# Half-sequence loads, mask constants copied one pair at a time, and zero matmuls in TensorE's gaps, in an attention and MLP kernel ordered by a planner

## The chip, the core and the metric

One core of one Trainium2 chip. The core has five instruction queues that run side by side and meet through semaphores: TensorE (PE, matmuls and transposes), VectorE (DVE), ScalarE (ACT), GpSimd (POOL) and SyncE (SP, which here only issues DMAs). Each queue is in order: an instruction that waits holds everything behind it. The metric is the device time of one execution in microseconds (us).

## What is computed

Chunked top-k causal attention over 4 batches of 8 heads (768 positions, 64 wide), followed by an MLP with ELU over the 3072 tokens. The softmax's maximum and the small constant in its divisor are left out here.

```python
ub  = sum(maximum(q * k_min, q * k_max))         # bound of each query against 24 chunks of 32 keys
sel = the 6 chunks with the largest ub that are not in the future
p   = exp(scale * q @ k.T) where sel and causal, else 0
x   = (p / p.sum()) @ v                          # heads side by side: [3072, 512]
h   = x @ w_in                                   # [3072, 2048]
g   = where(h > 0, h, exp(min(h, 0)) - 1)
out = g @ w_out                                  # [3072, 512]
```

## The kernel before

The work is cut by batch b (4), half of the queries h (2 halves of 384) and head pair r (4). For each (b, h, r) the function `prep` loads keys, queries and values, transposes them on PE (f32, three 128x128 transposes, L435), takes minimum and maximum of the keys per chunk on DVE (L454, tile kmm) and from them the operand kst (L469, L476), and writes the transposed keys and queries as bf16 into the tiles lhs and rhs. `select` then works on two pairs at once: four f32 matmuls give ub (L525), DVE transposes it (L536), finds the sixth largest per query (L545), compares (L551), transposes back (L557) and writes the result into the upper half of rhs (L565). The upper half of lhs holds constants, the same for every pair: the tile econst is copied into it by DVE (L418, one copy of 64x1536 for each of the eight lhs buffers). So one score matmul (L591) gives scores and mask together. ACT takes the exponential (L603, L609; tile pt), DVE multiplies the diagonal blocks by a triangle (L618, L626), PE multiplies by v (L645), DVE normalises (L656, L659), PE transposes (L670) and DVE stores the tile xt (L675). Four tiles xt, one for each pair, are the input of one MLP stage of 384 tokens.

An MLP stage has 16 first matmul groups (L687, four matmuls of 384 columns each), an exponential on ACT (L695), a subtraction on POOL (L699, tile m), a combination on DVE (L703, tile gT), and 3 x 16 second matmuls of 512 columns (L714), evicted by ACT (L722) and stored by SP. There are eight such stages, and attention of later halves runs between them.

Loads in before: batch 0 comes as half sequences (96 KB for one head of one tensor), batches 1 to 3 as whole ones (192 KB for keys and queries, 384 KB for two heads of values). There are three buffers each for keys, queries and values, each for a whole sequence of a pair, so the keys of a fourth pair wait until both halves of the first have been transposed. SP issues them, and also the stores, in one queue; the first queries go through ACT's queue. The weights come in eight DMAs on POOL's queue (L323, L329), each planned behind one of the casts of v on POOL (L502), which a table W_GATE names.

The order of instructions on every queue is made at build time by a small planner (`Graph.run`): it walks through modelled time, with a cost in ns for each operation and engine, and lets each engine take the available operation with the smallest `prio`. `prio` is a due time in us: attention of a half, its preparation PREPAHEAD earlier, its loads LOADAHEAD earlier still, the MLP stages by MLP0 and MLPW. The kernel then emits instructions in the planned order. At the start, 28 matmuls of 128 columns on a tile of zeros (L299) stand ahead of everything on PE.

Of the kernel before, what the change touches and what calls it, by code (L numbers as in the profile page):

```python
# [20 lines left out]
D = 64  # L21
# [6 lines left out]
P = 128  # L28
# [11 lines left out]

class Buf:
# [14 lines left out]
class Op:  # L56
    __slots__ = ("name", "engines", "emit", "deps", "nexts", "bufs", "prio", "seq", "wait",
                 "ready", "start", "finish", "engine", "xfer", "gate")


class Graph:
# [13 lines left out]
    def op(self, name, engines, emit, reads=(), writes=(), prio=0.0, xfer=None, after=()):  # L75
# [5 lines left out]
        o.gate = None  # L81
# [20 lines left out]
    def run(self, at=None, dma_lat=(900.0, 1500.0)):  # L102
# [6 lines left out]
        dma_free = 0.0  # L109
# [7 lines left out]
        while left:  # L117
# [5 lines left out]
            while events and events[0] <= t:  # L123
                heapq.heappop(events)
            while arriving and arriving[0][0] <= t:
# [4 lines left out]
            while moved:  # L130
                moved = False
                for e in engines:
# [28 lines left out]
                    o.engine, o.start = e, t  # L161
                    at[e] = t + dur
                    if o.xfer is not None:
                        begin = max(t + dur + dma_lat[0], dma_free)
                        dma_free = begin + o.xfer
                        o.finish = dma_free + dma_lat[1]
                    else:
                        o.finish = t + lat
                    heapq.heappush(events, at[e])
                    for b in o.bufs:  # L170
# [4 lines left out]
                        b.left -= 1  # L175
                        b.end = max(b.end, o.finish + SEM)
                        if b.cls == "bank":
                            b.used[e] = o.finish + SEM
                            heapq.heappush(events, o.finish + SEM)
                        if b.left == 0 and b.cls in free:  # L180
                            free[b.cls].append((b.end, b.slot))
                            heapq.heappush(events, b.end)
                    for n in o.nexts:
                        n.wait -= 1
                        n.ready = max(n.ready, o.finish + SEM)
                        if n.wait == 0:
                            heapq.heappush(arriving, (n.ready, n.seq, n))
                            heapq.heappush(events, n.ready)
# [33 lines left out]
def kernel(  # L222
# [30 lines left out]
    for h in range(2):  # L253
        slots(f"rhs{h}", 5, [P, 2, HS], BF16)
# [117 lines left out]
    def load(b, h, r, prio):  # L372
# [19 lines left out]
        if h == 0:  # L392
            vfs[b, r] = g.buf("vf")
# [388 lines left out]
```

## Time and profile before

| | before |
|---|---|
| time, median of 3 runs | 320.09 us (318.78 to 321.11) |
| the profiled execution, its own time | 321.54 us |
| its span, first to last instruction | 319.6 us |
| PE / DVE / ACT / POOL busy | 92% / 72% / 63% / 44% of the span |
| first MLP matmul (L687) starts | 51.44 us |
| moved by DMA | 29.78 MB |

Busy times are sums of recorded lengths; matmuls are pipelined, so two records overlap and a busy PE is not a PE at its peak. The granted clock (PEclk) is 1.00 at 2.4 GHz and 0.50 at 1.2 GHz. Ahead of its first change it has no record and is shown as 1.00.

### The profile page before, as it was taken

How to read it: one execution, taken by the hardware profiler on the slowest of the kernel's cores; microseconds unless marked ns; L12 is line 12 of the kernel's file. 1: busy time of each engine (PE TensorE's matmuls, PEld its weight loads, DVE VectorE, ACT ScalarE, POOL GpSimd, SP SyncE). 2: the span in 40 equal slices, each digit the busy share in tenths (PEclk: the TensorE clock that was granted, in tenths of full speed). 3: DMA queues.
4: the chain of work that ended last, by engine and by line, in shares of the span. 5: the costliest groups of instructions: out<-in, count | busy, mean ns of one | idle time of the engine just before them, and what ended most of it. 6: DMA issues, size and time to landing. Idle time of an engine off the chain costs nothing.

```text
span 319.6 us, 6664 instructions
## 1 busy us (share of the span) xinstructions
PE 293.0 (92%) x2278; PEld 177.5 (56%) x2300; DVE 229.0 (72%) x687; ACT 201.5 (63%) x438; POOL 142.1 (44%) x298
## 2 busy tenths in 40 slices
PE   7486679899899999999999999999999999899995
PEld 6252346566457466565674655666665556564642
DVE  8986569977949846885499838977599919751730
ACT  4352489587468288687585766785676655952722
POOL 8563436773457224671286105451284304420730
PEclk9997699999999999999999999999999999999999
DMA  8899999993428466100144335000330000001002
GB/s 168 184 195 194 211 198 192 205 198 70 100 68 194 88 164 151 34 2 33 68 99 100 83 84 131 2 2 35 105 62 0 35 33 36 0 2 66 35 0 98
DMA packets 83168, 29.78 MB, mean 93 GB/s; under 512 B 75968, under 2 KB 80064, under 8 KB 83136
## 3 DMA queue, kind: packets, MB, share of 16 engines
q1 hardware_dynamic: 77312, 24.78, 33.3%
q0 software_dynamic: 4224, 4.19, 8.8%
q10 hardware_dynamic: 1600, 0.39, 0.6%
q8 instruction: 18, 0.29, 0.4%
q14 instruction: 14, 0.11, 0.1%
HBM read 27.26 MB, written 6.29 MB: 105 GB/s over the span
## 4 chain that ended last, share of the span: by engine, by line
PE 56%; DVE 35%; ACT 3%; issue 2%; POOL 2%; POOLq 0%; ACTq 0%; DVEq 0%
PE bank L714 23%; PE bank L687 13%; PE bank L591 9%; DVE gT L703 8%; DVE kmm L454 5%; PE bank L645 4%; PE bank L525 4%; DVE thr L545 3%; PE bank L435 2%; DVE rhs L565 2%; DVE lhs L418 2%; ACT pt L603 2%; DVE kst L476 2%; DVE qr L492 2%; DVE ubT L536 2%
## 5 line engine op out<-in xcount | busy, mean ns | idle before, releaser
L699 POOL TENSOR_SCALAR m<-e 128x384 f32<-128x384 f32 x128 | 66.1, 523 | 78.3 <-ACT e L695 57.4
L603 ACT ACTIVATE pt<-bank 128x384 bf16<-128x384 f32 (+1 forms) x160 | 74.9, 542 | 35.0 <-PE bank L591 34.2
L687 PE MATMUL bank<-xt,w_in_sb 128*128 128x384 bf16 x512 | 93.2, 326 | 0.2
L714 PE MATMUL bank<-w_out_sb,gT 128*128 128x512 bf16 x362 | 91.4, 379 | 1.1
L703 DVE SCALAR_TENSOR_TENSOR gT<-bank,m 128x384 bf16<-128x384 f32 x128 | 67.6, 548 | 23.7 <-POOL m L699 22.0
L695 ACT ACTIVATE e<-bank 128x384 f32<-128x384 f32 x128 | 61.8, 499 | 31.4 <-PE bank L687 24.5
L687 PEld LDWEIGHTS <-w_in_sb 128*128 128x128 bf16 x512 | 48.7, 98 | 30.3 <-issue 1.9
L591 PE MATMUL bank<-rhs,lhs 128*128 128x384 bf16 (+2 forms) x288 | 55.5, 302 | 10.8 <-DVE rhs L565 6.3
L714 PEld LDWEIGHTS <-gT 128*128 128x128 bf16 x384 | 36.1, 98 | 34.3 <-issue 0.8
L445 POOL COPY lhs<-kt 64x384 bf16<-64x384 bf16 x59 | 31.8, 540 | 27.5 <-ACT kt L441 25.0
L591 PEld LDWEIGHTS <-lhs 128*128 128x128 bf16 x288 | 26.9, 101 | 27.7 <-issue 11.8
L454 DVE TENSOR_REDUCE kmm<-bank 128x12 f32<-128x384 f32 x64 | 33.4, 545 | 4.5 <-PE bank L435 3.4
L645 PEld LDWEIGHTS <-pt 128*128 128x128 bf16 x672 | 24.8, 98 | 8.4 <-issue 2.7
L722 ACT ACTIVATE o<-bank 128x512 f32<-128x512 f32 x23 | 13.8, 600 | 23.4 <-PE bank L714 19.8
L645 PE MATMUL bank<-vext,pt 128*128 128x65 bf16 x672 | 26.7, 194 | 1.2 <-DVE pt L626 1.0
L441 ACT ACTIVATE kt<-bank 128x384 bf16<-128x384 f32 x29 | 14.5, 500 | 15.7 <-PE bank L435 13.1
L445 POOL CAST rhs<-qt 64x384 bf16<-64x384 f32 x21 | 11.3, 538 | 28.8 <-ACT qt L441 19.9
L525 PE MATMUL bank<-qt,kst 128*64 128x192 f32 (+1 forms) x64 | 17.5, 474 | 6.3 <-DVE kst L476 6.2
L618 DVE TENSOR_TENSOR pt<-pt,tri 128x512 bf16<-128x512 bf16 x32 | 14.6, 455 | 10.7 <-ACT pt L603 10.7
L441 ACT ACTIVATE rhs<-qt 64x384 bf16<-64x384 f32 x40 | 20.8, 521 | 1.5 <-DVE qt L443 0.9
L609 ACT ACTIVATE pt<-bank 128x512 bf16<-128x512 f32 x32 | 19.5, 608 | 1.9 <-PE bank L591 1.8
L435 PE MATMUL bank<-ident_f,qf 128*128 128x128 f32 x96 | 17.6, 298 | 1.0 <-POOL tri L308 0.6
(58 smaller groups left out, 280.0 us busy)
## 6 DMA issues: line engine op xcount, KB each, us to landing
out_dram<-o SPq DMA_DIRECT2D x24, 256.0 KB, 2.0
kf<-in_k_dram SPq DMA_DIRECT2D x24, 192.0 KB, 3.3
qf<-in_q_dram SPq DMA_DIRECT2D x24, 192.0 KB, 3.6
vf<-in_v_dram SPq DMA_DIRECT2D x12, 384.0 KB, 4.9
w_in_sb<-in_moe_w_in_dram POOLq DMA_DIRECT2D x4, 512.0 KB, 6.2
w_out_sb<-in_moe_w_out_dram POOLq DMA_DIRECT2D x4, 512.0 KB, 7.8
kf<-in_k_dram SPq DMA_DIRECT2D x16, 96.0 KB, 2.9
vf<-in_v_dram SPq DMA_DIRECT2D x16, 96.0 KB, 3.1
```

The source lines that it names most:

```text
L441: nc.scalar.activation(out=dst(), in_=src(), func=AF.Copy)
L445: nc.gpsimd.tensor_copy(out=dst(), in_=src())
L454: nc.vector.tensor_reduce(out=ap(kmm)[:, w, :], in_=ap(bank)[:, 0:HS].rearrange("p (c w) -> p c w", w=CHUNK), axis=AX.X, op=op)
L525: nc.tensor.matmul(ap(bank)[64 * j:64 * j + 64, 0:nq], lhsT=ap(ks[b, r])[:, w].rearrange("p h c -> p (h c)"), rhs=ap(qq[b, h, r][w])[:, q0 ...
L591: nc.tensor.matmul(ap(banks[hd])[:, o + pc:o + pc + wd], lhsT=ap(ls)[:, hd, P * kb:P * (kb + 1)], rhs=ap(rs)[:, hd, c0 - HS * h:c0 - HS * ...
L603: lambda e, hd=hd, pt=pt, banks=banks, wtot=wtot: nc.scalar.activation(out=ap(pt)[:, hd, 0:wtot], in_=ap(banks[hd])[:, 0:wtot], func=AF.Ex ...
L645: nc.tensor.matmul(o3v()[:, hd, qi, :], lhsT=ap(pt)[:, hd, P * qi + off:P * qi + off + P], rhs=ap(vx[b, r])[:, kb, hd, :], start=(kb == 0) ...
L687: nc.tensor.matmul(ap(bank)[:, 0:HS], lhsT=w_in_sb[:, kk, P * fc:P * (fc + 1)], rhs=ap(xT[b, h, kk]), start=(kk == 0), stop=(kk == NKK - 1))
L695: lambda e, eb=eb, bank=bank: nc.scalar.activation(out=ap(eb), in_=ap(bank)[:, 0:HS], func=AF.Exp),
L699: lambda e, eb=eb, mb=mb: nc.gpsimd.tensor_scalar(out=ap(mb), in0=ap(eb), scalar1=-1.0, scalar2=1.0, op0=AOT.add, op1=AOT.mult),
L703: lambda e, gt=gt, bank=bank, mb=mb: nc.vector.scalar_tensor_tensor(out=ap(gt), in0=ap(bank)[:, 0:HS], scalar=0.0, in1=ap(mb), op0=AOT.max ...
L714: nc.tensor.matmul(ap(bank), lhsT=ap(gts[fc])[:, P * tt:P * (tt + 1)], rhs=w_out_sb[:, fc, :], start=(fc == 0), stop=(fc == NFC - 1))
```

## The change

**Loads.** All keys, queries and values come as half sequences of one pair, for every batch, into 6, 5 and 7 half-size buffers, and v is cast half by half. SP's queue holds 212 DMAs instead of 128.

**Mask constants.** One of two memsets of econst goes; both selections on POOL read the same half. A copy of econst into a pair's lhs is now planned behind the kst operation of the last pair but one, instead of as early as possible.

**Zero matmuls.** The 28 at the start go. Fifty operations of two 128x512 matmuls on zeros, with the lowest priority of all, are given to the planner, which puts one wherever modelled PE has nothing else.

**The planner's model.** DMA queues now share the transfer rate, and POOL holds up DVE (and DVE POOL) where both use the port to SBUF that they share: all POOL operations, and those of DVE marked port=True. Start times, costs, buffer counts and due times change with it (table T). What each engine's instructions compute stays the same.

The diff, cut to its core:

```diff
+T = dict(kf=6, qf=5, vf=7, pt=12, xt=12, gT=26, qt=3, qr=3, rhs=5, nfirst=2, vlate=4.17,
+         gate=[1, 2, 3, 4, 5, 5, 8, 11], attw=[10.3, 19.0], mlp=[14.0, 15.1], loada=18.12,
+         prepa=9.74, sela=2.41, fill=50)
...
+                    if e == POOL or (e == DVE and o.port):
+                        held = max(0.0, port_free[DVE if e == POOL else POOL] - t)
+                        dur, lat = dur + held, lat + held
+                        port_free[e] = t + dur
...
-    slots("kf", 3, [P, 6, 2, D], F32)
-    slots("qf", 3, [P, 6, 2, D], F32)
-    slots("vf", 3, [P, 2, 6, D], F32)
+    slots("kf", T["kf"], [P, 3, 2, D], F32)
+    slots("qf", T["qf"], [P, 3, 2, D], F32)
+    slots("vf", T["vf"], [P, 3, 2, D], F32)
...
-    zeros = const.tile([P, P], BF16, name="zeros")
+    zeros = const.tile([P, 512], BF16, name="zeros")
...
-        nc.vector.memset(econst[up, 0], MASKNEG)
         nc.vector.memset(econst[up, 1], MASKNEG)
-        for i in range(FILL):
-            nc.tensor.matmul(store["bank"][7][:, 0:P], lhsT=zeros, rhs=zeros, start=True, stop=True)
...
-            nc.gpsimd.affine_select(out=econst[up, hd], in_=econst[up, hd],
+            nc.gpsimd.affine_select(out=econst[up, hd], in_=econst[up, 1],
...
-             writes=[(fixed, ("wi", i))], prio=-1.0, xfer=3400.0, after=[casts[W_GATE[i]]])
+             writes=[(fixed, ("wi", i))], prio=-1.0, xfer=3400.0,
+             after=[casts[W_GATE[i] - 1]] if W_GATE[i] else [])
...
-    FILL = 28
-    AT = {PE: 3500.0, ACT: 800.0, DVE: 3200.0, POOL: 6000.0, SP: 800.0}
-    W_GATE = [2, 3, 4, 5, 6, 7, 8, 9]
+    AT = {PE: 1300.0, ACT: 800.0, DVE: 4200.0, POOL: 5600.0, SP: 800.0}
+    W_GATE = T["gate"]
...
-    LOADAHEAD = 14.0
-    PREPAHEAD = 7.0
+    LOADAHEAD = T["loada"]
+    PREPAHEAD = T["prepa"]
...
     def load(b, h, r, prio):
-        if h == 0:
-            kfs[b, r], qfs[b, r] = g.buf("kf"), g.buf("qf")
-        kf, qf = kfs[b, r], qfs[b, r]
-        first = b == 0 and h == 0 and r < 2
+        kf, qf, vf = g.buf("kf"), g.buf("qf"), g.buf("vf")
+        first = b == 0 and h == 0 and r < T["nfirst"]
         ts = slice(HS * h, HS * (h + 1))
-        for buf, src, late in ((kf, k, 0.0), (qf, q, 0.001)):
+        for buf, src, late in ((kf, k, 0.0), (qf, q, 0.001), (vf, v, T["vlate"])):
             for hd in range(2):
-                if b == 0:
-                    dma(lambda buf=buf, src=src, hd=hd: (
-                            ap(buf)[:, 3 * h:3 * h + 3, hd],
-                            src[b, 2 * r + hd, ts].rearrange("(n p) d -> p n d", p=P)),
-                        [(buf, (h, hd))], [], (-100.0 + r) if first else prio + late, 440.0,
-                        f"ld{b}{h}{r}", eng=ACT if first and late else SP)
-                elif h == 0:
-                    dma(lambda buf=buf, src=src, hd=hd: (
-                            ap(buf)[:, :, hd],
-                            src[b, 2 * r + hd].rearrange("(n p) d -> p n d", p=P)),
-                        [(buf, (hh, hd)) for hh in range(2)], [], prio + late, 880.0, f"ld{b}{r}",
-                        issue=900.0)
-        if h == 0:
-            vfs[b, r] = g.buf("vf")
-        vf = vfs[b, r]
-        if b == 0:
-            for hd in range(2):
-                dma(lambda hd=hd: (ap(vf)[:, hd, 3 * h:3 * h + 3],
-                                   v[b, 2 * r + hd, ts].rearrange("(n p) d -> p n d", p=P)),
-                    [(vf, (h, hd))], [], prio + 3.0, 440.0, f"ldv{b}{h}{r}")
-        elif h == 0:
-            dma(lambda: (ap(vf).rearrange("p g n d -> p (g n) d"),
-                         v[b, 2 * r:2 * r + 2].rearrange("g s d -> (g s) d")
-                         .rearrange("(m p) d -> p m d", p=P)),
-                [(vf, (hh, hd)) for hh in range(2) for hd in range(2)], [], prio + 3.0, 1760.0,
-                f"ldv{b}{r}", issue=900.0)
+                early = first and src is not v
+                dma(lambda buf=buf, src=src, hd=hd: (
+                        ap(buf)[:, :, hd], src[b, 2 * r + hd, ts].rearrange("(n p) d -> p n d", p=P)),
+                    [(buf, hd)], [], (-100.0 + r) if early else prio + late, 450.0,
+                    f"ld{b}{h}{r}", eng=ACT if early and late else SP)
...
-                g.op("ec" + tag, {DVE: (480, 560)}, ec, writes=[(lb, "e")],
-                     prio=prio + 0.5)
+                g.op("ec" + tag, {DVE: (480, 560)}, ec, writes=[(lb, "e")], port=True,
+                     prio=prio + 0.5, after=[ecs[-2]] if len(ecs) > 1 else [])
...
-        def cast(name, ks_, cost, keys):
-            casts.append(g.op(
-                name, cost,
-                lambda e: nc.gpsimd.tensor_scalar(
-                    out=ap(vx[b, r])[:, ks_, :, 0:D].rearrange("p k g d -> p g k d"),
-                    in0=ap(vf)[:, :, ks_], scalar1=1.0, scalar2=0.0, op0=AOT.mult, op1=AOT.add),
-                reads=[(vf, key) for key in keys], writes=[(vx[b, r], hh) for hh in {k_[0] for k_ in keys}],
-                prio=prio + 3.0))
-        if b == 0:
-            cast("v" + tag, slice(3 * h, 3 * h + 3), {POOL: (520, 580)}, [(h, 0), (h, 1)])
-        elif h == 0:
-            cast("v" + tag, slice(0, 6), {POOL: (850, 910)}, [(hh, hd) for hh in range(2) for hd in range(2)])
+        casts.append(g.op(
+            "v" + tag, {POOL: (520, 580)},
+            lambda e: nc.gpsimd.tensor_scalar(
+                out=ap(vx[b, r])[:, 3 * h:3 * h + 3, :, 0:D],
+                in0=ap(vf), scalar1=1.0, scalar2=0.0, op0=AOT.mult, op1=AOT.add),
+            reads=[(vf, 0), (vf, 1)], writes=[(vx[b, r], h)], prio=prio + T["vlate"]))
...
+    last = None
+    for i in range(T["fill"]):
+        bank = g.buf("bank")
+
+        def fill(e, bank=bank):
+            for _ in range(2):
+                nc.tensor.matmul(ap(bank), lhsT=zeros[:, 0:P], rhs=zeros, start=True, stop=True)
+        last = g.op("fill", {PE: (432, 600)}, fill, writes=[(bank, 0)], prio=1e6,
+                    after=[last] if last else [])
```

DVE's queue behind the memsets of the constants, before: copies of econst, then qr (positive part of the queries), kmm (chunk minimum and maximum of the keys) and kst.

```order
L418 COPY lhs_81<-econst 64x1536
L418 COPY lhs_82<-econst 64x1536
L418 COPY lhs_83<-econst 64x1536
L418 COPY lhs_84<-econst 64x1536
L418 COPY lhs_85<-econst 64x1536
L418 COPY lhs_86<-econst 64x1536
L418 COPY lhs_87<-econst 64x1536
L492 TENSOR_SCALAR qr_122<-qt_118 128x192
L454 TENSOR_REDUCE kmm_115<-bank_62 128x12 x2
L418 COPY lhs_88<-econst 64x1536
L476 TENSOR_TENSOR kst_107<-kmm_115,half 128x4x12
```

The same place after the change.

```order
L437 COPY lhs_90<-econst 64x1536
L437 COPY lhs_91<-econst 64x1536
L462 COPY qt_127<-bank_68 128x384
L474 TENSOR_REDUCE kmm_124<-bank_67 128x12 x2
L513 TENSOR_SCALAR qr_130<-qt_127 128x192
L462 COPY qt_128<-bank_64 128x384
L496 TENSOR_TENSOR kst_116<-kmm_124,half 128x4x12
L474 TENSOR_REDUCE kmm_125<-bank_63 128x12 x2
L513 TENSOR_SCALAR qr_131<-qt_128 128x192
L489 TENSOR_TENSOR kmm_125<-kmm_125 128x12
L474 TENSOR_REDUCE kmm_126<-bank_61 128x12
```

Two copies instead of seven stand ahead of the first kmm, and a copy of transposed queries out of PSUM (qt) has come to DVE.

PE's queue behind the first zero matmuls, before: transposes of queries and keys (qf, kf) of three pairs, then the first selection matmuls.

```order
L435 MATMUL bank_61<-ident_f,qf_72 128x128 x3
L435 MATMUL bank_62<-ident_f,kf_69 128x128 x3
L435 MATMUL bank_63<-ident_f,qf_73 128x128 x3
L435 MATMUL bank_64<-ident_f,kf_70 128x128 x3
L435 MATMUL bank_65<-ident_f,kf_71 128x128 x3
L435 MATMUL bank_66<-ident_f,qf_74 128x128 x3
L525 MATMUL bank_67<-qt_118,kst_107 64x192
L525 MATMUL bank_67<-qt_119,kst_108 64x192
```

The same place after the change: zero matmuls stand between the transposes (each with its weight load).

```order
L454 MATMUL bank_67<-ident_f,kf_69 128x128 x3
L454 MATMUL bank_68<-ident_f,qf_75 128x128 x3
L762 LDWEIGHTS zeros
L762 MATMUL bank_61<-zeros 128x512
...
L762 LDWEIGHTS zeros
L762 MATMUL bank_62<-zeros 128x512
...
L454 MATMUL bank_63<-ident_f,kf_70 128x128 x3
L454 MATMUL bank_64<-ident_f,qf_76 128x128 x3
```

Ahead of the first MLP matmul there are 82 zero matmuls of 512 columns now; up to that point PE's queue has 48 transposes instead of 60, 36 score matmuls instead of 48 and 48 matmuls with v instead of 78.

The last second matmuls (L714, L731 after the change) of the program, before.

```order
L714 LDWEIGHTS gT_170
L714 MATMUL bank_64<-w_out_sb,gT_170 128x512
L714 LDWEIGHTS gT_171
L714 MATMUL bank_64<-w_out_sb,gT_171 128x512
L714 LDWEIGHTS gT_188
L714 MATMUL bank_64<-w_out_sb,gT_188 128x512
L714 LDWEIGHTS gT_189
L714 MATMUL bank_64<-w_out_sb,gT_189 128x512
```

Near the same place after the change.

```order
L731 LDWEIGHTS gT_177
L731 MATMUL bank_66<-w_out_sb,gT_177 128x512
L731 LDWEIGHTS gT_178
L731 MATMUL bank_66<-w_out_sb,gT_178 128x512
L762 LDWEIGHTS zeros
L762 MATMUL bank_63<-zeros 128x512
...
L731 LDWEIGHTS gT_195
L731 MATMUL bank_66<-w_out_sb,gT_195 128x512
```

Two zero matmuls stand behind each of the first three groups of four of the last sixteen, six in all, and twelve more behind the last one.

## Rows read from the trace of the kernel before

**Rows 1.** The page's first part, all engines: busy us, share of the span, instructions.
```profile
PE 293.0 (92%) x2278; PEld 177.5 (56%) x2300; DVE 229.0 (72%) x687; ACT 201.5 (63%) x438; POOL 142.1 (44%) x298
```

**Rows 2.** Busy time by stretch up to the first L687; columns as in the first line.
```profile
core 0: us, PE busy (x) PEld busy (x) DVE busy (x) ACT busy (x) POOL busy (x), PEclk, DMA share, GB/s
...
26.75:30.17 3.42, 3.42 (x8) 0.97 (x6) 0.47 (x2) 0.00 (x0) 1.76 (x4) 0.50 1.08 201
...
33.58:40.41 6.83, 5.63 (x24) 3.34 (x24) 3.25 (x8) 3.49 (x8) 2.77 (x5) 0.50 1.27 211
...
sum 51.44, PE 36.35 PEld 24.20 DVE 39.28 ACT 26.07 POOL 26.72; mean PE 6.06 PEld 4.03 DVE 6.55 ACT 4.35 POOL 4.45
```

**Rows 3.** The same view for stretches behind 64 us.
```profile
64.00:305.32 241.32, 234.81 (x1894) 142.55 (x1914) 175.65 (x524) 164.44 (x361) 103.70 (x210) 1.00 0.29 69
305.32:315.88 10.56, 10.47 (x49) 4.61 (x47) 1.67 (x3) 1.79 (x4) 1.07 (x3) 1.00 0.13 50
315.88:319.60 3.72, 0.00 (x0) 0.00 (x0) 0.00 (x0) 0.60 (x1) 0.00 (x0) 1.00 0.18 70
```

**Rows 4.** Timeline of PE and DVE, 0 to 52.2 us: start, length, instructions [idle before].
```profile
1.06 3.17 PE L299 MATMUL bank<-zeros 128*128 128x128 bf16 x28 [1.06 <-DVE warm L292]
...
4.80 5.66 DVE L418 COPY lhs<-econst 64x1536 bf16<-64x1536 bf16 x7
...
10.65 1.01 DVE L454 TENSOR_REDUCE kmm<-bank 128x12 f32<-128x384 f32 x2
...
19.02 2.29 PE L591 MATMUL bank<-rhs,lhs 128*128 128x384 bf16 x10 [1.36 <-DVE rhs L565]
...
22.17 0.84 PE L435 MATMUL bank<-ident_f,kf 128*128 128x128 f32 x3
...
23.42 0.53 PE L435 MATMUL bank<-ident_f,qf 128*128 128x128 f32 x3
...
51.44 1.07 PE L687 MATMUL bank<-xt,w_in_sb 128*128 128x384 bf16 x4
...
51.80 0.34 DVE L675 COPY xt<-bank 128x384 bf16<-128x384 bf16 x1
```

**Rows 5.** Waits of DVE up to 52.2 us: us in total, times, longest.
```profile
DVE ubT L536 <- PE bank L525: 5.6, 2, 3.1
```

**Rows 6.** Groups by line and shape, DVE: busy us, mean ns | idle before.
```profile
L454 DVE TENSOR_REDUCE kmm<-bank 128x12 f32<-128x384 f32 x64 | 33.4, 545 | 4.5 <-PE bank L435 3.4 <-ACT kt L441 0.9
...
L659 DVE TENSOR_TENSOR on<-bank,rcp 128x384 bf16<-128x384 f32 x32 | 17.4, 548 | 0.3
...
L618 DVE TENSOR_TENSOR pt<-pt,tri 128x512 bf16<-128x512 bf16 x32 | 14.6, 455 | 10.7 <-ACT pt L603 10.7
...
L443 DVE CAST rhs<-qt 64x384 bf16<-64x384 f32 x3 | 2.0, 653 | 0.0
...
L297 DVE MEMSET econst<- 64x768 bf16 x1 | 0.7, 698 | 0.1
```

**Rows 7.** Chain that ended last, pieces in order of time: start, us, what.
```profile
101.96 0.66 PE bank L435 x6
...
295.73 9.75 PE bank L687 x60
...
305.75 10.11 PE bank L714 x46
```

**Rows 8.** Waits of PE from 64 us on: us in total, times, longest.
```profile
PE bank L525 <- DVE kst L476: 1.7, 2, 1.1
```

**Rows 9.** DMA: the page's issues (KB, us to landing), SP's timeline and waits.
```profile
kf<-in_k_dram SPq DMA_DIRECT2D x24, 192.0 KB, 3.3
...
w_out_sb<-in_moe_w_out_dram POOLq DMA_DIRECT2D x4, 512.0 KB, 7.8
kf<-in_k_dram SPq DMA_DIRECT2D x16, 96.0 KB, 2.9
...
12.21 1.02 SPq L369 DMA_DIRECT2D kf<-in_k_dram  x2
...
SPq L369 <- ACT o L722: 134.3, 19, 24.9
```

More of the change, by code (lines that the diff above doesn't have):

```diff
@@ L57 @@
     __slots__ = ("name", "engines", "emit", "deps", "nexts", "bufs", "prio", "seq", "wait",
-                 "ready", "start", "finish", "engine", "xfer", "gate")
+                 "ready", "start", "finish", "engine", "xfer", "port")
 class Graph:
@@ L73, in buf, with op @@
         return Buf(cls)
-    def op(self, name, engines, emit, reads=(), writes=(), prio=0.0, xfer=None, after=()):
+    def op(self, name, engines, emit, reads=(), writes=(), prio=0.0, xfer=None, after=(),
+           port=False):
         o = Op()
@@ L80, in op @@
         o.start = o.finish = o.engine = None
-        o.gate = None
+        o.port = port
         for b, key in reads:
@@ L108, in run @@
         arriving = []
-        dma_free = 0.0
+        rings = {e: [] for e in (SP, ACT, POOL)}
+        dma_at, asked = 0.0, -1.0
+        port_free = {DVE: 0.0, POOL: 0.0}
         for o in self.ops:
@@ L174, in run @@
                             b.slot = fl.pop(k)[1]
[L175 to L188, printed above, removed]
+                    if o.xfer is None:
+                        o.finish = t + lat
+                        settle(o)
+                    else:
+                        rings[e].append([t + dur + dma_lat[0], o.xfer, o])
+                        heapq.heappush(events, t + dur + dma_lat[0] + o.xfer)
                     order.append(o)
@@ L470, in sub @@
                               op=AOT.subtract)
-        g.op("ks" + tag, {DVE: (85, 160), POOL: (200, 260)}, sub, reads=[(kmm, 0)], writes=[(kmm, 1)],
-             prio=prio)
+        g.op("ks" + tag, {DVE: (75, 150), POOL: (200, 300)}, sub, reads=[(kmm, 0)], writes=[(kmm, 1)],
+             prio=prio, port=True)
         def pad(e):
@@ L621, in tri @@
                         .to_broadcast([P, 2, 2, P]), op=AOT.mult)
-                g.op("tri" + tag, {DVE: (340, 430)}, tri, reads=[], writes=[(pt, 0), (pt, 1)], prio=pr)
+                g.op("tri" + tag, {DVE: (340, 430)}, tri, reads=[], writes=[(pt, 0), (pt, 1)], prio=pr,
+                     port=True)
             elif dg:
@@ L629, in tri @@
                         op=AOT.mult)
-                g.op("tri" + tag, {DVE: (200, 290)}, tri, reads=[], writes=[(pt, 0), (pt, 1)], prio=pr)
+                g.op("tri" + tag, {DVE: (200, 290)}, tri, reads=[], writes=[(pt, 0), (pt, 1)], prio=pr,
+                     port=True)
             for (kb, c0, wd, pc) in segs:
```

100 lines of the change are left out of this document (70 added, 30 removed).

## Prediction

> **What bounds the kernel now.** I read the engine shares first, then the spans of the first 51 us, then of the rest, and then the waits of the engines that wait or are waited for. TensorE (PE) is busy 92% of the span, VectorE (DVE) 72%, ScalarE (ACT) 63%, GpSimd (POOL) 44% [rows 1]. The share alone hides that there are two kernels here. From 64.00 to 305.32 us PE is idle for 241.32 - 234.81 = 6.5 us in all, and the last stretch of second matmuls (305.32 to 315.88) is busy to 0.1 us; then 3.7 us of eviction and store follow [rows 3]. There the kernel is bound by PE, and nothing short of less matmul work moves it by more than these 6.5 us. The first 51.44 us are different: the first MLP matmul (L687) starts only then [rows 4], because its four tiles xt need attention of all four head pairs of the first half sequence. Up to there PE was busy 36.35 us and DVE 39.28 us [rows 2].
>
> Two things lengthen that stage. First, the chain runs through DVE: seven copies of the mask constants take 4.80 to 10.46 us, and the first reduction of the transposed keys stands behind them in DVE's queue [rows 4]. Second, PE works at its half level. The granted clock reads 0.50 from 26.75 to 30.17 and from 33.58 to 40.41 [rows 2]. Ahead of the first change there is no record, but the durations tell: 28 filler matmuls of 128 columns need 3.17 us, 0.11 us each; three f32 transposes need 0.84 us at 22.17 and 0.53 us at 23.42 [rows 4]. So PE was at 1.2 GHz until about 23.3, with a little work and many gaps, and rose after it had worked nearly without a break from 19.02. The page on TensorE in the Trainium skill ("TensorE: Matmul & The Clock Gate", "What's actually happening") says the same: the throttled level is the default, and activity lifts it. The trace agrees.
>
> **The change, part by part: DVE's way to the last xt.** In before, DVE had done 39.3 us of work by 51.44 and 0.8 us more when the fourth xt was done at 52.14 [rows 2, 4]: 40.1. Its order is fixed, so the list up to the fourth xt can be compared item by item. After the change it holds four mask copies instead of eight (4 x 5.66/7 = 3.2 us less), no casts of q where there were two (2 x 0.653 = 1.3), one memset of 0.70 us less, two L618 products less (0.9), and one each less of L454 and L659 (0.55 each) [rows 4, 6]; a few smaller differences, on balance in the same direction, are left out. That is 7.2 us less: 32.9 us of work. To it come the waits. Before had 52.14 - 40.1 = 12.0 us of them, of which 5.6 us were two waits for the selection matmuls (L525) [rows 5], both while the clock was 0.50 [rows 2]. In the new order some 2.5 us of DVE work stands between the operands of the first selection and its transpose, so I let these 5.6 us go, and keep the other 6.4. So the last xt is done at 32.9 + 6.4 = 39.3. Twelve score matmuls (L591) of the next half stand ahead of the first L687, so I put that at **40.0 instead of 51.44: -11.4 us**. Bounds, with the same 0.7 us behind xt: at 3.4 us of waits it starts at 37.0 (-14.4), and with all 12.0 us of before at 45.6 (-5.8).
>
> **The filler matmuls.** 82 matmuls of 128x512 on zeros stand in front of the first L687. At the spacing of the last second matmuls, 10.11/46 = 0.22 us [rows 7], they are 17.7 us of PE. With the 15.2 us of real work left there, PE is filled for 34 of the 40 us. Each us that PE begins at the half level adds half a us. That fits under the 40.0, so I cost them at nothing; what hides them is DVE's work, and if that cover is gone each costs its 0.22 us. What they buy is the clock, which is in the waits above. Six more stand between the groups of the last sixteen second matmuls. There PE had no gap (10.47 of 10.56 busy [rows 3]), so these cost their full length: 6 x 0.22 = **+1.3 us** (bounds 0, if a gT comes late there, and 1.3). The last twelve run beside the final eviction and store, in which PE idled 3.72 us [rows 3]: 2.6 us, hidden.
>
> **Work that is now done later.** Ahead of the first L687 stand 12 f32 transposes fewer, 8 score matmuls of 384 columns, 30 matmuls of probabilities with v, and a few short ones. At 0.11 us each [rows 7], 0.1625 us (the L687 row, also 384 columns [rows 7]) and an estimated 0.03 us (65/512 of the 0.22 us row) that is 1.3 + 1.3 + 0.9, with the short ones about **+4.0 us** that PE does later, in the part where it has no slack.
>
> **The full stretch.** PE's waits for DVE there are few: 1.7 us for kst is the largest [rows 8]. Prep work gets 9.74 instead of 7 us of lead and the planner now counts the port that DVE and POOL share, so I take **-2.0 us** of the 6.5 (bounds -6 and +3: a new order can also lose).
>
> **Loads.** Loads of half a sequence double the number from batch 1 on: 212 on SP's queue where there were 128. An issue of two 96 KB loads takes 1.02 us [rows 9], so 84 more are some 43 us on SP, which spends 134 us waiting for ACT's evictions ahead of its stores [rows 9]; hidden, and if that cover went they would come on top of the queue. Landing took 2.9 us for 96 KB and 3.3 us for 192 KB, both far under the lead that the buffers give [rows 9]. A rule that speaks against this part stands in "DMA: Bandwidth & Descriptors", "Rules for kernel authors": join small transfers into large ones. By the rows the sum has nothing for the halving; by the rule the second rival below, at 319.5, would be the likelier. POOL's 12 more casts of v and ACT's 11 more copies of q lie on engines at 44% and 63%.
>
> **Sum.** -11.4 + 4.0 + 1.3 - 2.0 = -8.1 us. The profiled execution had a span of 319.6 us and 321.54 us in all; the median of the runs was 320.09, 1.45 less. So the span should be 311.5 and the time **312.0 us**.
>
> **The rivals.** *DVE never waits* (chance 0.17): first L687 at 37.0, and 4 us of the 6.5 gone: -14.4 + 4.0 + 1.3 - 4 = -13.1, 307 us. For it: a clock at full level shortens every matmul that DVE waits for. Against: selections and exponentials still alternate between three engines.
>
> *Loads fall behind* (0.14): the DMA engines were taken, at a share of 1.08 and 1.27 in the two stretches of low clock [rows 2]. All eight weight loads must be in before the first MLP can finish, and each takes 7.8 us to land in this crowd [rows 9]. In PE's order the first matmul that needs the last of them stands behind some 24 us of matmuls after the first L687 (20 in before), counted with the spacings above: at 64 us instead of 71. If the pace of the loads sets the time, the gain of 8 us is waited away: about 319.5. Against it: POOL issues the weight loads earlier, and ahead of the last one stand only three quarters of batch 1's first half, not all of batch 1's keys and queries.
>
> *The clock stays low* (0.04), on the slower side. PE needs 17.7 + 15.2 us at full level from 1.1 on, 34.0. Each us at the half level does half a us, so with the first 28 us low the first L687 comes at 48, and 48 - 51.44 + 4.0 + 1.3 - 2 is zero: from there on the fillers make the kernel slower; with 40 us low it starts at 54 and the time is 326 us. For it: the fillers at the start of before did not lift the level. Against: the unbroken work from 19.02 on did [rows 4].
>
> *Loads behind stores* (0.05), slower too: SP's queue is in order, and loads of the next half stand behind stores that wait for ACT (134.3 us [rows 9]). With six buffers for keys the slack is large, but if in each of the seven later stages PE waits over 1.2 us for a load the gain is gone; at 1.6 us it ends at 323.
>
> **How the numbers follow.** My forecast has 0.60; alone it would reach from 308 to 316.5. A measurement of this kernel can tell about 1% from no change, 316.9 to 323.3. Faster: 0.60 + 0.17 = 0.77; same: 0.14; slower: 0.04 + 0.05 = 0.09. The range that leaves out no more than 2 in 10 reaches from under the first rival (its -13.1, and 1.5 more for stalls that vanish), 305.5, to the second, 319.5.
>
> **What would show it.** In the changed kernel's profile: the first reduction of keys on DVE near 7 us instead of 10.65; the granted clock at 1.00 wherever it has a record before 40 us; the first L704 (the old L687) at 37 to 45.6; DVE's wait for the selection matmuls under 2 us; six zero matmuls inside the last second matmuls with 0.22 us each; PE idle between the first 64 us and the tail at 1 to 9 us. I am wrong if the first MLP matmul is early and PE then waits for w_out or for keys, or if PE is filled but DVE is late by the old 12 us.

## The result and the profile after

The changed kernel takes 310.53 us (median; 309.59 to 311.63), the kernel before 320.6 us on the same chip: a ratio of 0.9696, with a 95% interval of 0.9642 to 0.9749. That is 10.1 us less; the forecast had 8.1 less and 312.0. Ratios here and below leave out executions over 1.5% above the fastest of their kernel, which are one each of e2 and e7 and two of e6, its profiled one among them. The profiled execution took 310.68 us, with a span of 308.6 instead of 319.6.

The total was right by luck: the two largest terms behind it were not, and their errors cancel. From the start to the first MLP matmul I had expected 11.4 us less and it became 2.6 (48.80 instead of 51.44). Behind it I had expected 2.0 us fewer stalls, and some 13.4 went. Here is how that is read.

The page of the changed kernel, engine shares and the chain that ended last:

```profile
PE 295.0 (96%) x2346; PEld 178.3 (58%) x2372; DVE 221.6 (72%) x676; ACT 204.2 (66%) x449; POOL 143.5 (46%) x309
...
PE 87%; DMA 7%; SPq 5%; issue 1%
```

Busy time by stretch, same kernel (columns as in [rows 2]); the third row answers to the first of [rows 3]:

```profile
6.03:40.17 34.14, 24.09 (x173) 14.69 (x176) 21.82 (x72) 16.48 (x35) 18.80 (x42) 1.00 1.12 196
40.17:43.58 3.41, 3.41 (x33) 1.73 (x30) 0.80 (x3) 0.23 (x1) 1.26 (x4) 0.50 0.81 184
64.00:304.92 240.92, 239.65 (x1944) 146.21 (x1965) 174.91 (x522) 168.59 (x372) 106.97 (x224) 1.00 0.29 74
304.92:308.60 3.68, 2.75 (x13) 1.08 (x11) 0.00 (x0) 0.60 (x1) 0.00 (x0) 1.00 0.18 71
```

PE is idle for 1.3 us behind 64 us, where it was 6.5. From 6.03 to 40.17 it is idle for 10 of 34.14 us, zero matmuls included among its work. What it waited for, over the whole span (us in total, times, longest):

```profile
PE bank L454 <- DMA kf<-in_k_dram: 6.0, 2, 3.1
PE bank L454 <- DMA qf<-in_q_dram: 3.9, 1, 3.9
PE bank L762 <- DVE warm L336: 1.3, 1, 1.3
PE bank L731 <- issue: 0.2, 1, 0.2
```

Three waits for keys and queries, 9.9 us, all before the first MLP matmul; before, no load stood among PE's large waits. The timeline of PE (start, length, instructions [idle before]) has them in place, with the first MLP matmul and the tail:

```profile
18.30 0.52 PE L454 MATMUL bank<-ident_f,kf 128*128 128x128 f32 x3 [2.92 <-DMA kf<-in_k_dram]
...
27.89 0.52 PE L454 MATMUL bank<-ident_f,kf 128*128 128x128 f32 x3 [3.07 <-DMA kf<-in_k_dram]
...
38.80 0.52 PE L454 MATMUL bank<-ident_f,qf 128*128 128x128 f32 x3 [3.90 <-DMA qf<-in_q_dram]
...
48.80 1.46 PE L704 MATMUL bank<-xt,w_in_sb 128*128 128x384 bf16 x8
...
301.03 0.59 PE L762 MATMUL bank<-zeros 128*128 128x512 bf16 x2
301.46 1.03 PE L731 MATMUL bank<-w_out_sb,gT 128*128 128x512 bf16 x4
```

PE takes its instructions in order. The transposes (L454) of later pairs stand ahead of score matmuls whose operands are there, so a late load stops all of PE, and DVE behind it. DVE's waits up to 52.2 us, with the row that answers to [rows 5] first:

```profile
DVE ubT L551 <- PE bank L540: 5.5, 2, 5.2
DVE rcp L673 <- PE bank L662: 5.5, 3, 4.8
DVE pt L633 <- ACT pt L618: 3.7, 2, 3.0
```

**Where the stalls behind the first MLP matmul went.** Busy time doesn't show them all: a record of L704 lasts 326 ns (page after; 95.8 us for 512), while such matmuls follow each other every 0.1625 us [rows 7], so records overlap and cover small gaps. I therefore count spacings. Before, 512 first matmuls (0.1625 us each), 384 second ones (0.216), 132 f32 transposes (0.109), 240 score matmuls (22.1, 5.7 and 2.9 us by width), the selections (14.9), 594 with v (0.0295) and 81 transposes of attention (0.056) follow the first L687: 248.1 us. From there to the end of the last second matmul (its start and one spacing) it took 264.2. So PE lost some 16.2 us, where the gaps between records add up to 7.8 (6.5 of them behind 64 us). After: 252.1 of work, 1.3 of zero matmuls, 256.1 elapsed, 2.8 lost. The table has the same count for every profiled run. It is an estimate from spacings, all at the full clock level; its columns add up to the span within 0.2 us. *Rest* is what follows the last second matmul.

| kernel | first MLP matmul at | work behind it | zeros | PE lost | rest | span | median us |
|---|---|---|---|---|---|---|---|
| before | 51.44 | 248.1 | 0 | 16.2 | 4.0 | 319.6 | 320.1 |
| changed | 48.80 | 252.1 | 1.3 | 2.8 | 3.7 | 308.6 | 310.5 |
| e1 late weights | 41.16 | 252.1 | 1.3 | 3.7 | 3.7 | 301.9 | 303.7 |
| e2 no zeros in the tail | 45.24 | 252.1 | 0 | 2.8 | 3.7 | 303.8 | 307.3 |
| e3 no zeros | 50.03 | 252.1 | 0 | 2.8 | 3.7 | 308.6 | 309.7 |
| e4 no hold on the port | 33.85 | 254.7 | 1.3 | 13.7 | 9.3 | 312.7 | 313.5 |
| e5 old due times | 46.07 | 253.7 | 1.3 | 7.9 | 4.1 | 313.0 | 313.6 |
| e6 e1 + e2 | 39.23 | 252.1 | 0 | 8.8 | 3.7 | 303.8 | 304.1 |
| e7 e1 + e3 | 39.31 | 252.1 | 0 | 2.8 | 3.7 | 297.9 | 302.8 |
| e8 before + hold | 43.33 | 249.8 | 0 | 9.2 | 4.0 | 306.3 | 308.9 |
| e9 e7, no hold | 33.57 | 254.7 | 0 | 11.6 | 3.7 | 303.5 | 304.9 |
| e10 before + copies gated | 42.50 | 250.1 | 0 | 17.2 | 4.0 | 313.8 | 315.7 |
| e11 before + due times | 41.15 | 250.7 | 0 | 12.3 | 4.3 | 308.4 | 309.7 |
| e12 before + 140 zeros | 51.51 | 248.1 | 0 | 16.1 | 4.0 | 319.6 | 321.5 |

### The profile page after: what moved, and what is told of

The parts are those of the page before. It is cut to its first block, busy times and chain, and to the rows that moved or that the text cites. A ratio compares the mean times of both kernels' runs of the same rounds, so it can differ in the third digit from the quotient of the medians.

```text
span 308.6 us, 6957 instructions
## 1 busy us (share of the span) xinstructions
PE 295.0 (96%) x2346; PEld 178.3 (58%) x2372; DVE 221.6 (72%) x676; ACT 204.2 (66%) x449; POOL 143.5 (46%) x309
## 4 chain that ended last, share of the span: by engine, by line
PE 87%; DMA 7%; SPq 5%; issue 1%
PE bank L704 27%; PE bank L731 26%; PE bank L606 11%; PE bank L662 7%; PE bank L454 6%; PE bank L540 6%; SPq L411 5%; DMA qf<-in_q_dram 4%; DMA kf<-in_k_dram 3%; PE bank L762 2%; PE bank L687 2%
## 5 line engine op out<-in xcount | busy, mean ns | idle before, releaser
L704 PE MATMUL bank<-xt,w_in_sb 128*128 128x384 bf16 x512 | 95.8, 326 | 0.0
L731 PE MATMUL bank<-w_out_sb,gT 128*128 128x512 bf16 x362 | 92.0, 379 | 1.2 <-issue 0.2
L618 ACT ACTIVATE pt<-bank 128x384 bf16<-128x384 f32 (+1 forms) x160 | 76.6, 538 | 18.3 <-PE bank L606 18.0
L704 PEld LDWEIGHTS <-w_in_sb 128*128 128x128 bf16 x512 | 48.7, 98 | 28.6 <-issue 0.6
L464 POOL COPY lhs<-kt 64x384 bf16<-64x384 bf16 x62 | 32.7, 527 | 60.1 <-ACT kt L460 58.1
L731 PEld LDWEIGHTS <-gT 128*128 128x128 bf16 x384 | 35.9, 98 | 32.5 <-issue 0.6
L606 PE MATMUL bank<-rhs,lhs 128*128 128x384 bf16 (+2 forms) x288 | 54.4, 290 | 0.1
L606 PEld LDWEIGHTS <-lhs 128*128 128x128 bf16 x288 | 25.8, 98 | 19.0 <-issue 1.7
L739 ACT ACTIVATE o<-bank 128x512 f32<-128x512 f32 x23 | 13.7, 595 | 30.5 <-PE bank L731 28.9
L460 ACT ACTIVATE kt<-bank 128x384 bf16<-128x384 f32 x32 | 15.8, 494 | 23.6 <-PE bank L454 22.8
L460 ACT ACTIVATE rhs<-qt 64x384 bf16<-64x384 f32 x51 | 26.7, 523 | 4.3 <-DVE qt L462 3.5
L662 PEld LDWEIGHTS <-pt 128*128 128x128 bf16 x672 | 24.6, 99 | 8.1 <-issue 4.7
L762 PE MATMUL bank<-zeros 128*128 128x512 bf16 x96 | 26.9, 410 | 1.4 <-DVE warm L336 1.3
L662 PE MATMUL bank<-vext,pt 128*128 128x65 bf16 x672 | 26.6, 195 | 0.0
L454 PE MATMUL bank<-ident_f,kf 128*128 128x128 f32 x96 | 15.9, 274 | 6.0 <-DMA kf<-in_k_dram 6.0
L522 POOL TENSOR_SCALAR vext<-vf 128x384 bf16<-128x384 f32 x32 | 17.2, 543 | 8.6 <-DMA vf<-in_v_dram 4.0
```

The source lines that it names most:

```text
L454: nc.tensor.transpose(ap(bk)[:, P * n:P * (n + 1)], ap(src)[:, n], ident_f)
L460: nc.scalar.activation(out=dst(), in_=src(), func=AF.Copy)
L606: nc.tensor.matmul(ap(banks[hd])[:, o + pc:o + pc + wd], lhsT=ap(ls)[:, hd, P * kb:P * (kb + 1)], rhs=ap(rs)[:, hd, c0 - HS * h:c0 - HS * ...
L618: lambda e, hd=hd, pt=pt, banks=banks, wtot=wtot: nc.scalar.activation(out=ap(pt)[:, hd, 0:wtot], in_=ap(banks[hd])[:, 0:wtot], func=AF.Ex ...
L662: nc.tensor.matmul(o3v()[:, hd, qi, :], lhsT=ap(pt)[:, hd, P * qi + off:P * qi + off + P], rhs=ap(vx[b, r])[:, kb, hd, :], start=(kb == 0) ...
L704: nc.tensor.matmul(ap(bank)[:, 0:HS], lhsT=w_in_sb[:, kk, P * fc:P * (fc + 1)], rhs=ap(xT[b, h, kk]), start=(kk == 0), stop=(kk == NKK - 1))
```

## Experiments on the start: loads, zero matmuls, clock

**e1, the weight loads later.** POOL issues the first weight load at 10.73 us in the changed kernel, at 16.69 before. In the stretch from 10 to 29 us loads of 96 KB landed slowly (DMA issues of the changed kernel in that stretch: KB, median us to landing):

```profile
w_in_sb<-in_moe_w_in_dram POOLq DMA_DIRECT2D x4, 512.0 KB, 8.2
w_out_sb<-in_moe_w_out_dram POOLq DMA_DIRECT2D x2, 512.0 KB, 9.6
vf<-in_v_dram SPq DMA_DIRECT2D x8, 96.0 KB, 7.1
kf<-in_k_dram SPq DMA_DIRECT2D x6, 96.0 KB, 5.9
qf<-in_q_dram SPq DMA_DIRECT2D x6, 96.0 KB, 6.4
```

From 64 to 290 us they take 2.4 to 2.6 us. So seven weight loads (the expectation says six) are moved later in POOL's order, five of them behind named casts of v, the last two behind another load and a kst operation:

```
 order = g.run(AT)
+for w, c in (("w_in0", "v003"), ("w_in1", "v010"), ("w_in2", "v011"), ("w_in3", "v012"),
+             ("w_out0", "v013"), ("w_out1", "w_out0"), ("w_out2", "kp013")):
+    o = next(x for x in order if x.name == w)
+    order.remove(o)
+    order.insert(next(i for i, x in enumerate(order) if x.name == c) + 1, o)
```

> The changed kernel with the same order on PE, DVE, ACT and SP; on POOL's queue six weight loads stand later (the first behind the cast of the fourth pair's v instead of the first pair's). Theory 'weights crowd the loads': in the changed kernel PE waited three times, 9.9 us in all, for keys and queries that took 6.2 to 10.1 us to land while weight loads were under way, against 2.4 to 2.9 without. These waits fall under 3 us in all, the first L704 comes at 40 to 43 us instead of 48.8, and the time at 302 to 305. Rival 'the loads' own pace is the limit' (SP issues one each 0.53 us): the waits stay above 8 us, the first L704 stays within 2 us of 48.8, the time within 309 to 312.

Measured: 303.70 us, ratio to before 0.949 (0.9435 to 0.9546). The first weight load is issued at 18.61, the first L704 starts at 41.16, and of PE's waits for loads one is left (waits of PE, e1, and from its timeline the first L704):

```profile
PE bank L454 <- DMA qf<-in_q_dram: 2.5, 1, 2.5
PE bank L762 <- DVE warm L336: 1.3, 1, 1.3
...
41.16 1.46 PE L704 MATMUL bank<-xt,w_in_sb 128*128 128x384 bf16 x8
```

The key loads of e1 issued from 10 to 18.6 us, ahead of its first weight load, and then from 18.6 to 29:

```profile
kf<-in_k_dram SPq DMA_DIRECT2D x4, 96.0 KB, 2.6
...
kf<-in_k_dram SPq DMA_DIRECT2D x4, 96.0 KB, 7.8
```

Queries went from 2.6 to 8.1 us, values from 2.6 to 6.3. So loads land as slowly beside the weights here; they are later ones, and PE stood still for only one of them. In this order of PE, the weights' early place cost the changed kernel 7 us. The Trainium skill has a rule beside this ("DMA: Bandwidth & Descriptors", "Issuing engines are not separate DMA queues"): transfers started by different engines run on the same 16 DMA engines and interleave. These rows agree.

**e2 and e3, the zero matmuls.** e2 drops those behind the last first matmul, e3 all 100:

```
 order = g.run(AT)
+last_mm = max(i for i, x in enumerate(order) if x.name.startswith("h7."))
+order = [x for i, x in enumerate(order) if x.name != "fill" or i < last_mm]    # e2
+order = [x for x in order if x.name != "fill"]                                 # e3
```

> The changed kernel without its 18 zero matmuls behind the last first matmul of the MLP (six inside the last second matmuls, twelve behind them). Theory: the six cost their full 0.216 us each, so 309.2 us (-1.3). Rival: they fill gaps that PE has anyway, no change (within 0.4 us of the changed kernel).

> The changed kernel with none of its 100 zero matmuls. Theory 'the fillers hold the clock': granted clock 0.50, or durations at the half level, over most of the stretch up to the first L704; the 15.2 us of real work in it take up to 30, the first L704 comes at 51 to 55 instead of 48.8, and with 1.3 us back in the tail the time is 311.5 to 315.5. Rival 'loads set the pace there, the clock does not matter': first L704 within 1 us of 48.8, time 309.2 (the tail alone).

Measured: e2 307.26 us (0.9580; 0.9527 to 0.9633), e3 309.71 (0.9653; 0.9589 to 0.9717). In e2 the way from the first L704 to the end is 258.5 us instead of 259.8: the tail's 1.3 us. The rest of its gain is the start, 45.24 instead of 48.80 with the very same order up to there. PE's waits for loads were 6.0 us instead of 9.9; so the landing of loads moves the start by several us between executions, and what starts less than that apart shows nothing. In e3 the half level lasts long: three f32 transposes take 0.85 to 0.90 us until the clock rises at 22.81 (0.49 to 0.55 in the changed kernel), and from there to 50.12 the granted clock averages 0.75. PE waits 12.4 us for loads, and the first L704 starts 1.2 us later. By the times, e2 and e3 differ by 2.4 us with intervals that overlap, so what the 82 early zero matmuls are worth here stays open.

**e6 and e7, both on top of e1.** With loads no longer in the way the clock could count again. e6 is e1 with e2's edit, e7 is e1 with e3's.

> The changed kernel with both things that the first runs showed to cost time taken out: weight loads later in POOL's order, and no zero matmuls behind the last first matmuls. Theory (the two are separate, 303.7 - 1.3): 302.4 us, range 301 to 303.5. Rival (the zero matmuls of the tail hide under another wait once the start is shorter): 303.7 as with the late loads alone.

> Weight loads late, and none of the 100 zero matmuls at all. Theory (with the loads early, loads set the pace of the start and the clock hardly counted; with the loads late PE's real work sets it, and the half level costs again): first MLP matmul at 44 to 48 us instead of 41.2, low clock until 20 us and longer; 305.5 to 309 us. Rival (the clock does not count here either): first MLP matmul at 40 to 42, 302.4 us or less.

Measured: e6 304.11 us (301.33 to 307.04; ratio 0.9425, 0.9377 to 0.9472), e7 302.82 (299.96 to 304.50; ratio 0.9426, 0.9369 to 0.9484), whose profiled execution is the 299.96. By the ratios they are the same, and neither is told from e1 (0.949). For e7 my theory fell and the rival held, but for 0.4 us in the time and 0.7 in the start. PE of e7:

```profile
4.26 0.88 PE L454 MATMUL bank<-ident_f,kf 128*128 128x128 f32 x3 [4.26 <-DMA kf<-in_k_dram]
...
20.93 0.85 PE L454 MATMUL bank<-ident_f,kf 128*128 128x128 f32 x3
...
24.67 0.49 PE L454 MATMUL bank<-ident_f,qf 128*128 128x128 f32 x3
...
39.31 1.46 PE L704 MATMUL bank<-xt,w_in_sb 128*128 128x384 bf16 x8
```

PE was at 1.2 GHz until after 20.93 us, and the first L704 came at 39.31 all the same, against 41.16 with 82 zero matmuls. So they buy no time that shows here: e7 is e6 without them, at the same ratio. The profiled execution of e6 took 305.93 us, so its row in the table (8.8 us lost) does not stand for the 0.9425.

**e12, zero matmuls in the kernel before.** 140 instead of 28 at the start:

```
-FILL = 28
+FILL = 140
```

> The kernel before, with 140 zero matmuls of 128 columns at its start instead of 28, and nothing else: they fill PE until the first keys and queries can be transposed and a little beyond. Theory of the forecast (PE at its half level lengthens the selections that DVE waits for): full level from some 6 us on instead of 23.3, first MLP matmul at 46 to 49 us, 315 to 318 us. Rival (loads and DVE set the pace at the start, the clock counts little): 319 us or more.

Measured: 321.52 us, 0.8% slower (1.008; 1.0047 to 1.0113). PE of e12:

```profile
1.06 9.57 PE L299 MATMUL bank<-zeros 128*128 128x128 bf16 x140 [1.06 <-DVE warm L292]
10.47 0.50 PE L435 MATMUL bank<-ident_f,qf 128*128 128x128 f32 x3
...
51.51 0.94 PE L687 MATMUL bank<-xt,w_in_sb 128*128 128x384 bf16 x4
```

The level did rise (0.50 us for three transposes instead of 0.87; the granted clock reads 1.00 from 4.42 us), and the first L687 stood where it was. As a trial of the clock alone it is not clean: the zeros also held the first transposes back from 4.79 to 10.47 us, and the level fell again at 18.1. That the clock buys nothing that shows at this start rests on e7 against e6.

## Experiments on the full stretch: the port, the due times, the mask copies

**e4 and e9, the changed kernel without the hold.** The planner no longer delays an operation for the port that DVE and POOL share; e4 is the changed kernel with this edit, e9 is e7 with it:

```
-held = max(0.0, port_free[DVE if e == POOL else POOL] - t)
+held = 0.0
```

> The changed kernel, planned without the hold of DVE and POOL on each other's port (one line of the planner), so in another order. Theory 'the port in the model took PE's stalls away': by the spacing of matmuls PE lost about 16.3 us between the first L687 and the last L714 in before and 2.7 us in the changed kernel; without the hold it loses 9 us or more there, and the time is 316 or more. Rival 'due times, buffers and half loads did it': PE loses under 5 us there, and the time is within 2 us of the changed kernel's 310.5.

> The version with late weight loads and no zero matmuls, with the planner's hold on the shared port taken out. In the earlier run without the hold 38 zero matmuls stood behind the last real one and made the run longer by themselves; here there are none, so the hold is priced cleanly. Theory (the hold takes PE's waits for DVE out): PE loses 7 us or more between first and last MLP matmul where it lost 2.8; 305.5 to 312 us. Rival (the hold buys nothing that an earlier start does not): 301.5 to 304.5 us.

Measured: e4 313.48 us (0.9789; 0.9747 to 0.9831). PE lost 13.7 us, as the theory had it, but the time is under the theory's 316 and over the rival's 312.5. Its tail and its start show that it priced something else too:

```profile
33.85 2.11 PE L704 MATMUL bank<-xt,w_in_sb 128*128 128x384 bf16 x12
...
303.48 8.37 PE L762 MATMUL bank<-zeros 128*128 128x512 bf16 x38
```

The planner had placed fewer zeros early and 38 were left for the end, some 5.6 us behind all other work (9.3 instead of 3.7 in the table). The start says more about e1. The first L704 comes 15 us earlier than in the changed kernel, although the first weight load is issued at 11.09 us, about as early, and keys issued from 10 to 29 us land in 7.4 us at the median. But 39 transposes stand ahead of it instead of 48, and 24 score matmuls instead of 36. PE waits 1.1 us for loads ahead of it, not 9.9. So slow loads need not delay the start: that depends on what stands behind them in PE's order. Hence e9, without zeros: 304.89 us (0.9550; 0.9511 to 0.9589), 2.1 us behind e7. PE lost 11.6 us instead of 2.8, as the theory wanted, and its waits for DVE are back (waits of PE in e9 from the first L704 to 300 us; e7 has none there):

```profile
PE bank L606 <- DVE gT L720: 1.5, 3, 0.7
PE bank L662 <- DVE pt L642: 1.4, 2, 0.8
PE bank L606 <- ACT kt L460: 0.9, 1, 0.9
```

But the first MLP matmul came 5.7 us earlier, with 2.6 us more work left. So the time, 304.9, lay between the theory (305.5 or more) and the rival (304.5 at most): the hold trades an early start for fewer stalls, and wins by 2 us here, or by 4 if the ratios to before are compared (0.9426 and 0.9550; e7 and e9 ran on two chips).

**e8, the hold alone in the kernel before.**

```
+port_free = {DVE: 0.0, POOL: 0.0}
...
+if e == POOL or (e == DVE and o.name.startswith(port)):
+    held = max(0.0, port_free[DVE if e == POOL else POOL] - t)
+    dur, lat = dur + held, lat + held
+    port_free[e] = t + dur
```

with port = ("ec", "ka", "ks", "kp", "qr", "qa", "lt", "mk", "tri"), the names that the change marks.

> The kernel before, with one part of the change alone: the planner holds an operation of POOL, or one of DVE that uses the shared port, until the other is done with it. Theory (that alone takes most of PE's waits for DVE out of the full stretch): of the 16.2 us that PE lost there, 6 to 12 go; 308 to 315 us. Rival (it needs the new due times or the new start): 317 us or more, with the waits for gT, xt, rhs and pt still there.

Measured: 308.87 us (0.9648; 0.9611 to 0.9685). These lines alone are worth as much as the whole change. Of the 16.2 us lost 7.0 went. PE's named waits from the first MLP matmul on fell only from 5.5 to 3.2 us (those for xt, rhs and gT are still there), so most of the 7.0 us is in stalls that no row names. The first MLP matmul came at 43.33 with 1.7 us more work behind it, although DVE's queue still begins with seven mask copies (DVE of e8):

```profile
4.80 4.73 DVE L424 COPY lhs<-econst 64x1536 bf16<-64x1536 bf16 x7
...
9.93 1.01 DVE L460 TENSOR_REDUCE kmm<-bank 128x12 f32<-128x384 f32 x2
```

**e5 and e11, the due times.** e5 gives the changed kernel the old ones; e11 gives the kernel before the new ones (the other entries of T are left out):

```
-vlate=4.17, attw=[10.3, 19.0], loada=18.12, prepa=9.74, sela=2.41
+vlate=3.0,  attw=[10.0, 19.0], loada=14.0,  prepa=7.0,  sela=2.0     # e5; e11 the other way
```

> The changed kernel with the due times of before (loads 14.0 us ahead instead of 18.12, preparation 7.0 instead of 9.74, selection 2.0 instead of 2.41, v 3.0 instead of 4.17 later, attention of the first halves 10.0 instead of 10.3 us wide); the planner still counts the port of DVE and POOL. Theory (the port in the planner takes PE's waits for DVE out of the full stretch): PE loses under 6 us there, as in the changed kernel; 309 to 312 us. Rival (the longer lead of the preparation does it): waits of PE for gT, xt, rhs and pt come back, 6 us or more; 314 to 320 us.

> The kernel before, with the new due times alone (loads 18.12 us ahead, preparation 9.74, selection 2.41 behind it, v 4.17, attention of first halves 10.3 wide), without the hold on the port. Theory (the lead alone also takes waits away, in the changed kernel it was worth some 5 us of PE's loss): PE loses 9 to 13 us behind the first MLP matmul instead of 16.2; 312 to 317 us. Rival (without the hold the planner thinks DVE is on time anyway, and three buffers of whole sequences give no more lead): 318.5 us or more.

Measured: e5 313.63 us (0.9785; 0.9727 to 0.9843), 3.1 us behind the changed kernel, with 7.9 us lost. The time lies between theory (312 at most) and rival (314 or more); the loss is of the rival's size, though the named waits that came back are mostly for ACT, not for DVE (waits of PE in e5 from the first L704 on):

```profile
PE bank L606 <- ACT pt L618: 1.5, 3, 0.7
PE bank L606 <- DVE rhs L580: 0.4, 1, 0.4
```

e11: 309.72 us (0.9714; 0.9670 to 0.9758), faster than its theory. The due times alone also bring nearly the whole gain: in the profiled execution 10.3 us from the earlier start, less 2.6 us of work moved behind it, and 3.9 us of the loss. With the hold and the due times both tried in both kernels, the rest of the change (buffers, half loads, costs, zero matmuls) shows little in the loss: 9.2 and 7.9 with the hold alone (e8, e5), 12.3 and 11.6 with the due times alone (e11, e9). The changed kernel without both was not run.

**e10, the mask copies alone.** From the third pair on a copy waits for the statistics (kst) of two calls earlier; the list ecs holds those operations (cut to the core):

```
-g.op("ec" + tag, {DVE: (480, 560)}, ec, writes=[(lb, "e")], prio=prio + 0.5)
+g.op("ec" + tag, {DVE: (480, 560)}, ec, writes=[(lb, "e")], prio=prio + 0.5,
+     after=[ecs[-2]] if len(ecs) > 1 else [])
```

> The kernel before, with one part of the change alone: from the third pair on a mask copy waits for the block statistics (kst) of two calls earlier, so two copies stand at the start of DVE's queue instead of seven. Theory (the copies hold up the first key reduction and with it the start): first reduction near 7 us, first MLP matmul 2 to 4 us earlier than 51.4; 316 to 318.5 us. Rival (the copies fill time in which DVE would have waited): 319 to 321 us.

Measured: 315.73 us (0.9880; 0.9832 to 0.9929), 0.3 us under the theory's range and clear of the rival. DVE of e10:

```profile
4.80 1.11 DVE L419 COPY lhs<-econst 64x1536 bf16<-64x1536 bf16 x2
...
6.79 1.02 DVE L455 TENSOR_REDUCE kmm<-bank 128x12 f32<-128x384 f32 x2
```

The first reduction starts at 6.79 and the first MLP matmul at 42.50, 8.9 us earlier instead of the 2 to 4 expected; but 2.0 us of work and 1.0 us of stalls move behind it. 5.8 us are left of the span, and 3.2 in the medians. The start of the MLP is not the end of the kernel, and a new order does not lower the loss by itself: it is 17.2 here.

## Why the prediction came out right, point by point

**What bounds the kernel.** Half right. The start and the full stretch do have different limits. But "nothing short of less matmul work moves it by more than these 6.5 us" failed: behind the first MLP matmul 13.4 us of stalls went with 5.3 us more for PE to do. The step that failed is taking PE's busy time as its work: a record of L704 lasts 326 ns at 162 ns of spacing. The Trainium skill ("Perfetto Trace Analysis", "Identifying the Most-Contended Engine") says that the busy share of matmuls is not a good measure of how close a kernel is to its limit (roofline), since they are pipelined. These rows agree.

**DVE's way to the last xt, -11.4.** Mis-sized, and outside its bounds: -2.6 in the profiled execution. The work was sized well (DVE was busy for 32.4 us in the first 48.80, I had 32.9; DVE's 0.8 us between 51.44 and 52.14 can only be 0.7, which changes nothing), and the first reduction came at 7.93. The waits failed. I let the 5.6 us behind the selections go and kept 6.4; in their place stand 5.5 us behind the selections and 5.5 more for L662, the longest of each behind PE's waits for loads at 38.80 and 27.89. So two of the signs that I had named did not come, the first L704 at 45.6 or earlier and a wait for the selections under 2 us. The earlier weight loads were in the diff; I set them down as an argument against the rival on loads and gave them no price. With the first weight load at 18.61 instead of 10.73 us (e1; 16.69 before) the size of the term holds: 41.16, or 39.31 in e7, for the 40.0 of the forecast.

**The zero matmuls.** That the 82 ahead of the MLP are hidden holds, and so do the 1.3 us of the tail (0.43 us for each pair; e2). That they buy time through the clock did not show: e7 against e6.

**Work done later, +4.0.** Held: 252.1 against 248.1, by the count of matmuls.

**The full stretch, -2.0.** Mis-sized. By the measure that it was given in, PE's idle time between records behind 64 us, it was -5.2 (6.5 to 1.3), within its bounds; by the spacings, which the time follows, -13.4, outside them. Both the hold and the due times feed it: with the hold alone the loss falls from 16.2 to 9.2 (e8), with the due times alone to 12.3 (e11); without the hold it is 11.6 (e9), with the old due times 7.9 (e5). The two do not add up in the total, since both shorten the same start.

**Loads.** That halving them is hidden held in so far as no load stands among PE's waits behind 48.80; no run halves them alone. The mechanism of the rival *loads fall behind* was real, but earlier than I had put it: keys and queries before the MLP, not the last weights at 64 us. *The clock stays low* and *loads behind stores* did not come; the granted clock read 0.50 only from 40.17 to 43.58, behind the longest wait.

**The sum.** -2.6 + 4.0 + 1.3 - 13.4 - 0.3 (the rest behind the last matmul) = -11.0, which is 308.6 - 319.6. The forecast's terms were off by +8.8 and -11.4: two errors that cancel, which is luck, and the time alone would not have shown either.

Three things stay open. Why the start before was as late as 51.44, when the hold (43.33), the copies (42.50) or the due times (41.15) each alone bring it 8 to 10 us forward, was not taken apart; each changes DVE's and PE's order. What moves the landing of loads between executions of one kernel (45.24 and 48.80 with one order) was not tried. How the hold takes the stalls away, by which operations it moves, was not followed through the order.

## What to carry to other kernels

Count matmuls times their spacing before calling TensorE full; busy time hides small stalls, here 16.2 us behind 7.8. When a change lets bulk loads start earlier, price every small load that shares the DMA engines with them and stands ahead of something in an in-order queue. And try each part alone: three parts were each worth 3 to 11 us in the kernel before, the whole change 10, and one more part, the earlier weight loads, cost 7 that no total shows.

## What the runs showed of the hardware

Beside the six weight loads of 0.5 MB issued from 10 to 29 us, loads of 96 KB landed in 5.9 to 7.1 us at the median, against 2.4 to 2.6 from 64 to 290 us and 2.6 in e1 from 10 to 18.6, ahead of its weights. I had counted such a load with 2.9 us [rows 9] everywhere; that row is of keys over the whole of before, where queries and values issued from 10 to 29 us, beside three weight loads, took 4.7 and 5.5.

The mask copy's time depends on what POOL does beside it. In e10 two take 1.11 us, while eight memsets of POOL in the same time take 2.38; in the changed kernel it is the other way round (timeline of DVE and POOL, changed kernel):

```profile
4.83 2.60 DVE L437 COPY lhs<-econst 64x1536 bf16<-64x1536 bf16 x2
4.91 1.22 POOL L354 MEMSET kst<- 128x128 f32 x8
```

A copy beside an idle POOL takes 0.55 us (before, from 8.97 on), and each of these memsets 0.20, so in each of the two kernels one waits for the other. The Trainium skill has this as an exclusive lock ("SBUF — State Buffer", "SBUF: two separate sides"): whichever starts first keeps the shared port pair for its whole instruction. The rows agree that one waits for the other. Which started first they do not settle: in both kernels a record of POOL is still open when the first copy's begins. A planner that counts it (e8) gained 11 us. It lost 7.0 us less to stalls; why its start came earlier is open.
